# Merging the inverted 32-blocks: four heads in one product of 128 rows instead of two heads in one of 64, for a linear-attention and mixture-of-experts kernel

## The chip, the cores and the metric

The kernel runs on one core of one Trainium2 chip, as a single program. The metric is the device time of an execution in microseconds (us); lower is better. The time of a kernel is the median of its runs.

## The reference

The reference has two parts. The first is a recurrence with a 40x40 state for each of 4 batches and 8 heads over 768 time steps, all in float32:

```python
for t in range(S):                                   # 768 steps
    y[:, :, t] = einsum('bhd,bhde->bhe', rt, state)
    Sa = einsum('bhde,bhe->bhd', state, at)
    state = state * wt[:, :, None, :] - einsum('bhd,bhe->bhde', Sa, bt) \
            + einsum('bhd,bhe->bhde', vt, kt)
```

The second takes its output as a matrix x of 3072 tokens by 320, computes gate logits `x @ w_gate` (320x8), turns their exponentials into a matrix P by eight rounds of row and column normalisation, and adds up, over 8 experts, `P[:, e] * (relu(x @ w1[e]) @ w2[e])` with a hidden width of 1024.

## The kernel before, in words

The kernel has two stages. `attention` computes the recurrence and writes x to device memory; `body` then runs the experts. Only `attention` is changed.

**Chunks.** Time is cut into 12 chunks of 64 steps (`NCH`, `C`). A chunk is handled for the 4 batches one after the other; the 8 heads of a batch are 4 pairs (`NP`), a pair occupying rows 0 to 39 and 64 to 103 of a tile. `prep` (L110) loads a chunk and batch, scales k, b and a by running products of the decay, forms the 64x64 matrices of inner products on TensorE (`ll`, L154) and writes the strictly triangular part that has to be inverted to device memory (`lt` to `ld`, L157 or L173).

**The inverse.** The recurrence inside a chunk needs, for each batch and head, the inverse T of a 64x64 unit triangular matrix. Chunks are taken in six groups of two (`GROUPS`). For a group, `load_lu` (L368) brings the two diagonal 32x32 blocks of all its matrices into VectorE's layout, `inv_diag` to `inv_16` invert them on VectorE, and `finish` (L362) writes the inverted blocks to device memory, straight (`ud`, L365) and transposed (`nd`, L366). The upper right 32x32 block of T is then the product of the first inverted block, the off-diagonal block and the second inverted block. This merge is what is changed.

**The merge.** `tload(c)` (L228) issues ten DMAs on SP's queue for a chunk: two for the off-diagonal blocks (`lb`, L238), two for the transposed first block (`t1`, L241), two for the second block (`t2`, L243), and four that put both inverted blocks on the diagonal of `tt` (L247). A pair of heads is held block-diagonally in 64 rows and 64 columns; 16 pairs (4 batches by 4 pairs) stand beside each other along the free axis. `tmat(c, half)` (L249) runs twice for a chunk, each time for 8 pairs, that is two batches: 8 products of a 64x64 stationary with 32 moving columns into `gp` (L256), two ScalarE copies from `gp` onto the diagonal of `gs` (L257, L258), 8 products of the same shape into `op` (L261), and two ScalarE copies into the upper right blocks of `tt` (L262, L263). `lb` and `gs` are the lower and the upper 64 partitions of one tile, and so are `t1` and `t2`.

**The recurrence.** `recur(c, b)` (L265) is a generator of five steps: products `av` (L283), `xc` (L291), `pu` (L302, whose stationary operand is `tt`), `c2` (L309), and the transpose `zt` (L329) of the new state, with VectorE, ScalarE and GpSimd work between them. `gate` (L336) adds the gate logits of a finished chunk, four products of 64 stationary and 8 moving columns (`lp`, L339), which `gate_step` (L347) puts between the `xc` products.

**The order.** Each piece of work gets a due time in a list `ev` (L378 to L412), and is emitted in the order of these times: step k of chunk c and batch b at 5c + k + 1.1b, `tload(c)` at 5c - 0.5, and `tmat` of the first half at 5c, of the second half at 5c + 2.2. Within the attention stage the framework then orders the instructions of each engine itself, from these priorities and from its own estimate of when each can start; from the ninth block of the experts on the order is the program's. Each engine works through its own queue in order. `gp`, `op` and `lp` share two accumulator banks (tag `pt`). `tt` has two buffers, the tile of `t1` and `t2` and that of `lb` and `gs` one each.

**The experts.** `layer1` (L579, products `p` at L577, hi and lo parts of split operands) and `layer2` (L634, products `op` at L642) run in 128 blocks; the change does not touch them.

Of the kernel before, what the change touches and what calls it, by code (L numbers as in the profile page):

```python
# [11 lines left out]
F32 = mybir.dt.float32  # L12
# [8 lines left out]
NP = 4  # L21
# [7 lines left out]
def attention(ctx, tc, d, xd, ps, pq, pt, gs, lg):  # L29
    nc = tc.nc  # L30
# [3 lines left out]
    const = ctx.enter_context(tc.tile_pool(name="a_const", bufs=1))  # L34
# [15 lines left out]
    for n in range(NCH * NB - NSX, NCH * NB):  # L50
        i, pool = n % NSX, sets[n - NCH * NB + NSX]
# [8 lines left out]
        bb_b[i] = pool.tile([128, NP, 104], F32, name=f"bb{i}")  # L60
        cc_b[i] = pool.tile([R2, NP], F32, name=f"cc{i}")
    tt_b = [const.tile([128, 4 * NP, 128], F32, name=f"tt{i}") for i in range(NTB)]
    td_b = [const.tile([128, 4 * NP, 32], F32, name="td")]
    lg_b = [const.tile([128, 4 * NP, 64], F32, name="lg")]
    ab_b = [pin.tile([R2, NP, 128], F32, name=f"ab{i}") for i in range(2)]
    g1_b = [pin.tile([R2, NP, 65], F32, name=f"g1{i}") for i in range(1)]
    vz_b = [const.tile([R2, NP, 104], F32, name=f"vz{i}") for i in range(5)]
    c1_b = [const.tile([R2, NP, 104], F32, name=f"c1{i}") for i in range(2)]
# [15 lines left out]
    def clear():  # L84
        nc.gpsimd.memset(unf, 0.0)
        nc.gpsimd.memset(unf[:, 0:1024:33], 1.0)
        nc.gpsimd.memset(tnf, 0.0)
        for t in vz_b + c1_b + lg_b:
            nc.vector.memset(t, 0.0)
        for t in tt_b:  # L90
            nc.gpsimd.memset(t, 0.0)
# [11 lines left out]
    def rot(key, lst):  # L103
        i = state[key]
        state[key] = (i + 1) % len(lst)
        return lst[i]
# [121 lines left out]
    def tload(c):  # L228
        tt = rot("tt", tt_b)
        tts[c] = tt  # L230
        ld, ud, nd = invs[GRP[c][0]]
        t1, t2, lb = td_b[0][0:64], td_b[0][64:128], lg_b[0][0:64]
        cc = GRP[c][1]
        q = [slice(h * 32, h * 32 + 32) for h in range(2)]
        u = [[slice(cc * 64 + blk * 32 + h * 16, cc * 64 + blk * 32 + h * 16 + 16) for h in range(2)]
             for blk in range(2)]
        for h in range(2):
            nc.sync.dma_start(out=lb[q[h], :, q[h]],  # L238
                              in_=ld[cc, 0:32].rearrange("j b p h s -> j (b p) h s")[:, :, h, 32:64])
        for h in range(2):  # L240
            nc.sync.dma_start(out=t1[q[h]], in_=nd[u[0][h]].rearrange("g j s -> j g s"))  # L241
        for h in range(2):
            nc.sync.dma_start(out=t2[q[h]], in_=ud[u[1][h]].rearrange("g j s -> j g s"))  # L243
        for h in range(2):
            for blk in range(2):
                r = slice(h * 64 + blk * 32, h * 64 + blk * 32 + 32)
                nc.sync.dma_start(out=tt[r, :, r], in_=ud[u[blk][h]].rearrange("g j s -> j g s"))  # L247

    def tmat(c, half):  # L249
        gl = slice(half * 8, half * 8 + 8)  # L250
        tt = tts[c][:, gl]
        t1, t2 = td_b[0][0:64, gl], td_b[0][64:128, gl]
        lb, gs = lg_b[0][0:64, gl], lg_b[0][64:128, gl]
        gp = pt.tile([64, 2 * NP, 32], F32, name="gp", tag="pt")
        for p in range(2 * NP):
            nc.tensor.matmul(gp[:, p], lhsT=lb[:, p], rhs=t1[:, p], start=True, stop=True)  # L256
        nc.scalar.copy(out=gs[0:32, :, 0:32], in_=gp[0:32])  # L257
        nc.scalar.copy(out=gs[32:64, :, 32:64], in_=gp[32:64])  # L258
        op = pt.tile([64, 2 * NP, 32], F32, name="op", tag="pt")
        for p in range(2 * NP):  # L260
            nc.tensor.matmul(op[:, p], lhsT=gs[:, p], rhs=t2[:, p], start=True, stop=True)  # L261
        nc.scalar.copy(out=tt[0:32, :, 32:64], in_=op[0:32])  # L262
        nc.scalar.copy(out=tt[64:96, :, 96:128], in_=op[32:64])  # L263

    def recur(c, b):  # L265
        pp = preps[c, b]
# [89 lines left out]
    preps, invs, tts = {}, {}, {}  # L356
# [33 lines left out]
    for c in range(NCH):  # L390
        for b in range(NB):
            for k in range(5):
                ev.append((5 * c + k + SKEW * b, step, (c, b)))
        t = 5 * c + 2 - T_LEAD
        ev.append((t - L_LEAD, tload, (c,)))
        for half in range(2):
            ev.append((t + 2 * SKEW * half, tmat, (c, half)))
    for s, cs in enumerate(GROUPS):
        us = slice(0, 64 * len(cs))
        t0 = 5 * cs[0] - 10  # L400
# [24 lines left out]
SKEW = 1.1  # L425
# [35 lines left out]
def body(ctx, tc, d, out):  # L461
# [377 lines left out]
```

## Time and profile before

| | us |
|---|---|
| median of 3 runs | 1874.04 |
| lowest, highest run | 1859.17, 1875.54 |
| the profiled execution | 1873.12 |
| its span, first to last instruction | 1871.3 |
| TensorE matmul busy | 1777.2 |
| VectorE busy | 1373.9 |
| ScalarE busy | 856.0 |
| GpSimd busy | 868.1 |

The span lies 1.8 us below the time of its own execution. PE is TensorE's matmuls, PEld its loads of the stationary operand, DVE VectorE, ACT ScalarE, POOL GpSimd, SP the engine that issues most DMAs. Every float32 product of the attention stage stands in the trace as two matmul instructions with a weight load each. A row of the timeline gives the start, the time from the first start to the last end, the engine, the line, the tiles, the shape (128*104 is 128 rows and 104 columns of the stationary operand; 128x104 after it is the moving operand) and the count of merged instructions. A matmul lasts 0.2 to 0.3 us from its start to its end, but the next can start much sooner, so the distance between starts is what a product costs. PEclk is the share of TensorE's clock that was granted.

### The profile page before, as it was taken

Reading aid. Unit: us, or ns where it says so; the run is one execution under the profiler, and the core shown is the slowest. Engines: PE = TensorE matmul, PEld = TensorE weight load, DVE = VectorE, ACT = ScalarE, POOL = GpSimd, SP = SyncE. Lnnn points to the kernel's source line nnn. Section 1 sums busy time; section 2 is a strip of 40 time slices with the busy share of each in tenths; the row PEclk is TensorE's granted clock in tenths of the full one; section 3 lists DMA queues with packets and bytes.
Section 4 is the critical chain, followed back from the end, with each engine's and each line's share of the span. In section 5 each row is a group of like instructions: output and inputs, shape, how many; then the busy total and the mean of one; then the engine's idle time right before and its main releaser. Section 6 shows DMA issues by size and latency. Waiting matters only on the chain.

```text
span 1871.3 us, 32059 instructions
## 1 busy us (share of the span) xinstructions
PE 1777.2 (95%) x12035; PEld 1735.4 (93%) x12035; DVE 1373.9 (73%) x2378; ACT 856.0 (46%) x1848; POOL 868.1 (46%) x849
## 2 busy tenths in 40 slices
PE   4479999999999999999999999999999999999999
PEld 4468889889988899999999999999999999999999
DVE  6885958756389877676877768886776867767675
ACT  6346767654563434344343434344343434434342
POOL 6544646431265337182643718005371835538170
PEclk8568989977879999999999999999999999999999
DMA  8477877873741111020111102211110201102011
GB/s 190 115 152 156 176 169 183 170 149 80 171 127 45 37 37 55 20 74 19 56 37 37 56 19 74 59 30 37 37 58 17 74 19 56 40 35 67 8 37 43
DMA packets 214048, 141.47 MB, mean 76 GB/s; under 512 B 177157, under 2 KB 191493, under 8 KB 213893
## 3 DMA queue, kind: packets, MB, share of 16 engines
q1 hardware_dynamic: 210693, 134.18, 28.1%
q10 hardware_dynamic: 3200, 5.25, 1.1%
q8 instruction: 95, 1.56, 0.4%
q14 instruction: 60, 0.49, 0.1%
HBM read 113.82 MB, written 25.56 MB: 74 GB/s over the span
## 4 chain that ended last, share of the span: by engine, by line
PE 77%; DVE 5%; DMA 3%; POOL 1%; issue 1%; SPq 1%; ACT 1%; DVEq 0%; POOLq 0%; ACTq 0%
PE op L642 35%; PE p L577 33%; PE xc L291 2%; PE pu L302 1%; PE av L283 1%; PE lp L339 1%; DVE hl L601 1%; PE c L309 1%; PE ll L154 1%; PE op L261 1%; PE gp L256 1%; DMA ld<-lt 1%; DMA inp<-in_inp_dram 1%; DVE sm L595 1%; PE zt L329 1%
## 5 line engine op out<-in xcount | busy, mean ns | idle before, releaser
L577 PE MATMUL p<-xch,wh 128*128 128x384 f32 (+1 forms) x1792 | 605.6, 339 | 6.1 <-DVE u L595 2.2
L598 ACT ACTIVATE hh<-sm 128x384 fp32r<-128x384 f32 x512 | 269.5, 527 | 728.9 <-DVE sm L595 728.9
L642 PE MATMUL op<-wh,hh 128*128 128x320 f32 x1536 | 476.8, 311 | 1.1 <-ACT hh L598 0.9
L642 PE MATMUL op<-wl,hh 128*128 128x320 f32 x1536 | 474.5, 309 | 0.0
L642 PE MATMUL op<-wh,hl 128*128 128x320 f32 x1536 | 467.6, 310 | 1.3 <-DVE hl L601 1.3
L523 POOL TENSOR_TENSOR wl<-ws,wh 128x640 fp32r<-128x640 f32 x60 | 103.1, 1718 | 605.9 <-ACT wh L521 605.7
L601 DVE SCALAR_TENSOR_TENSOR hl<-sm,hh 128x384 fp32r<-128x384 f32 x512 | 375.4, 766 | 2.7 <-ACT hh L598 2.2
L577 PEld LDWEIGHTS p<-xch,wh 128*128 128x128 f32 (+1 forms) x1792 | 337.2, 188 | 9.8 <-DVE u L595 3.8
L577 PE MATMUL p<-xcl,wh 128*128 128x384 f32 x896 | 302.6, 338 | 0.0
L577 PE MATMUL p<-xch,wl 128*128 128x384 f32 x896 | 301.9, 337 | 0.0
L642 PEld LDWEIGHTS op<-wh,hh 128*128 128x128 f32 x1536 | 290.2, 189 | 2.0 <-ACT hh L598 1.9
L642 PEld LDWEIGHTS op<-wl,hh 128*128 128x128 f32 x1536 | 291.0, 189 | 0.0
L642 PEld LDWEIGHTS op<-wh,hl 128*128 128x128 f32 x1536 | 286.9, 188 | 2.1 <-DVE hl L601 2.0
L595 DVE TENSOR_TENSOR sm<-p,u 128x384 f32<-128x384 f32 x384 | 234.5, 621 | 9.2 <-PE p L577 0.5
L577 PEld LDWEIGHTS p<-xcl,wh 128*128 128x128 f32 x896 | 168.7, 188 | 0.0
L577 PEld LDWEIGHTS p<-xch,wl 128*128 128x128 f32 x896 | 168.6, 188 | 0.0
L595 DVE TENSOR_TENSOR sm<-p,p 128x384 f32<-128x384 f32 x128 | 71.2, 557 | 128.6 <-PE p L577 71.9
L595 DVE TENSOR_TENSOR p<-p,p 128x384 f32<-128x384 f32 x128 | 71.1, 555 | 101.6 <-PE p L577 100.2
L313 POOL TENSOR_TENSOR y<-ws,gl 104x256 f32<-104x256 f32 x48 | 42.8, 892 | 153.9 <-DVE ws L311 92.2
L595 DVE TENSOR_TENSOR u<-p,p 128x384 f32<-128x384 f32 x128 | 70.8, 553 | 57.0 <-PE p L577 55.9
L531 POOL TENSOR_TENSOR wl<-ss,wh 128x512 fp32r<-128x512 f32 x60 | 90.4, 1506 | 29.0 <-ACT wh L528 24.8
L154 PE MATMUL ll<-ab,kb 104*128 104x128 f32 x336 | 61.7, 341 | 40.7 <-POOL kb L142 16.2
(161 smaller groups left out, 2823.8 us busy)
## 6 DMA issues: line engine op xcount, KB each, us to landing
ws<-in_wts_dram SPq DMA_DIRECT2D x60, 832.0 KB
inp<-in_inp_dram SPq DMA_DIRECT2D x42, 419.2 KB
rb<-in_r_dram SPq DMA_DIRECT2D x48, 208.0 KB
ld<-lt ACTq DMA_DIRECT2D x40, 128.0 KB
vz<-in_v_dram SPq DMA_DIRECT2D x48, 104.0 KB
gd<-g SPq DMA_DIRECT2D x48, 104.0 KB
gl<-gd SPq DMA_DIRECT2D x48, 104.0 KB
f<-in_vt_dram SPq DMA_DIRECT2D x48, 80.0 KB
```

Source lines behind the costliest of these rows:

```text
L154: nc.tensor.matmul(ll[:, p], lhsT=kb[:, p], rhs=ab[:, p], start=True, stop=True)
L256: nc.tensor.matmul(gp[:, p], lhsT=lb[:, p], rhs=t1[:, p], start=True, stop=True)
L261: nc.tensor.matmul(op[:, p], lhsT=gs[:, p], rhs=t2[:, p], start=True, stop=True)
L291: nc.tensor.matmul(xc[h][:, p], lhsT=pp["sx"][:, p, h], rhs=f[:, p, h], start=True, stop=True)
L313: nc.gpsimd.tensor_tensor(out=y, in0=ws[:, :, 0:64], in1=gl, op=ALU.mult)
L523: g.tensor_tensor(out=wl[:, 0:640], in0=raw[:, 256:896], in1=wh[:, 0:640], op=ALU.subtract)
L531: g.tensor_tensor(out=lv[:, 3:7], in0=so[:, :, 0], in1=hv[:, 3:7, 0], op=ALU.subtract)
L577: nc.tensor.matmul(o, lhsT=w_, rhs=x_, start=(j == 0), stop=(j == 3))
L595: eng.tensor_tensor(out=out, in0=x, in1=y, op=ALU.add)
L598: nc.scalar.activation(out=hh[:, f, h], in_=sm[f][:, h], func=AF.Relu)
L601: v.scalar_tensor_tensor(out=hl[:, f, h], in0=sm[f][:, h], scalar=0.0, in1=hh[:, f, h], op0=ALU.max, op1=ALU.subtract)
L642: nc.tensor.matmul(ops[i], lhsT=a[:, h, cs], rhs=w_[:, cw], start=(f == 0 and h == 0 and j == 0), stop=(last and h == 1 and j == 2))
```

## The change

The merge handles four heads in one product. A product now has a 128x128 block-diagonal stationary operand: four diagonal 32x32 blocks, namely two heads of a pair in batches 0 and 1 (x = 0) and the two heads of the pair with the same place in batches 2 and 3 (x = 1). Eight products instead of sixteen cover a chunk in each of the two steps, and `tmat(c)` runs once, at the due time of the former first half. The tiles `t1`, `t2` have 128 partitions and half as many columns; `lb` and `gs` are now one and the same tile, whose diagonal blocks are overwritten by the copies out of `gp`. Each of the two steps has four copies of the same size as before instead of two in each of two halves. `tload` issues sixteen DMAs instead of ten: twelve that carry half as much each in place of six, and the four of `tt` unchanged.

```diff
-    td_b = [const.tile([128, 4 * NP, 32], F32, name="td")]
-    lg_b = [const.tile([128, 4 * NP, 64], F32, name="lg")]
+    t1_t, t2_t = (const.tile([128, 2 * NP, 32], F32, name=x) for x in ("t1", "t2"))
+    lb_t = gs_t = const.tile([128, 2 * NP, 128], F32, name="lb")
...
     def tload(c):
...
-        for h in range(2):
-            nc.sync.dma_start(out=lb[q[h], :, q[h]],
-                              in_=ld[cc, 0:32].rearrange("j b p h s -> j (b p) h s")[:, :, h, 32:64])
-        for h in range(2):
-            nc.sync.dma_start(out=t1[q[h]], in_=nd[u[0][h]].rearrange("g j s -> j g s"))
-        for h in range(2):
-            nc.sync.dma_start(out=t2[q[h]], in_=ud[u[1][h]].rearrange("g j s -> j g s"))
+        lv = ld[cc, 0:32].rearrange("j b p h s -> j (b p) h s")
+        for x in range(2):
+            for h in range(2):
+                r = q[2 * x + h]
+                nc.sync.dma_start(out=lb_t[r, :, r], in_=lv[:, x * 8:x * 8 + 8, h, 32:64])
+        for t, src, blk in ((t1_t, nd, 0), (t2_t, ud, 1)):
+            for x in range(2):
+                for h in range(2):
+                    o = u[blk][h].start + x * 8
+                    nc.sync.dma_start(out=t[q[2 * x + h]], in_=src[o:o + 8].rearrange("g j s -> j g s"))
         for h in range(2):
             for blk in range(2):
                 r = slice(h * 64 + blk * 32, h * 64 + blk * 32 + 32)
                 nc.sync.dma_start(out=tt[r, :, r], in_=ud[u[blk][h]].rearrange("g j s -> j g s"))
 
-    def tmat(c, half):
-        gl = slice(half * 8, half * 8 + 8)
-        tt = tts[c][:, gl]
-        t1, t2 = td_b[0][0:64, gl], td_b[0][64:128, gl]
-        lb, gs = lg_b[0][0:64, gl], lg_b[0][64:128, gl]
-        gp = pt.tile([64, 2 * NP, 32], F32, name="gp", tag="pt")
+    def tmat(c):
+        tt = tts[c]
+        q = [slice(i * 32, i * 32 + 32) for i in range(4)]
+        gp = pt.tile([128, 2 * NP, 32], F32, name="gp", tag="pt")
         for p in range(2 * NP):
-            nc.tensor.matmul(gp[:, p], lhsT=lb[:, p], rhs=t1[:, p], start=True, stop=True)
-        nc.scalar.copy(out=gs[0:32, :, 0:32], in_=gp[0:32])
-        nc.scalar.copy(out=gs[32:64, :, 32:64], in_=gp[32:64])
-        op = pt.tile([64, 2 * NP, 32], F32, name="op", tag="pt")
+            nc.tensor.matmul(gp[:, p], lhsT=lb_t[:, p], rhs=t1_t[:, p], start=True, stop=True)
+        for r in q:
+            nc.scalar.copy(out=gs_t[r, :, r], in_=gp[r])
+        op = pt.tile([128, 2 * NP, 32], F32, name="op", tag="pt")
         for p in range(2 * NP):
-            nc.tensor.matmul(op[:, p], lhsT=gs[:, p], rhs=t2[:, p], start=True, stop=True)
-        nc.scalar.copy(out=tt[0:32, :, 32:64], in_=op[0:32])
-        nc.scalar.copy(out=tt[64:96, :, 96:128], in_=op[32:64])
+            nc.tensor.matmul(op[:, p], lhsT=gs_t[:, p], rhs=t2_t[:, p], start=True, stop=True)
+        for x in range(2):
+            for h in range(2):
+                nc.scalar.copy(out=tt[h * 64:h * 64 + 32, x * 8:x * 8 + 8, h * 64 + 32:h * 64 + 64], in_=op[q[2 * x + h]])
...
-        for half in range(2):
-            ev.append((t + 2 * SKEW * half, tmat, (c, half)))
+        ev.append((t, tmat, (c,)))
```

More of the change, by code (lines that the diff above doesn't have):

```diff
@@ L87, in clear @@
         nc.gpsimd.memset(tnf, 0.0)
-        for t in vz_b + c1_b + lg_b:
+        for t in vz_b + c1_b + [lb_t]:
             nc.vector.memset(t, 0.0)
@@ L231, in tload @@
         ld, ud, nd = invs[GRP[c][0]]
-        t1, t2, lb = td_b[0][0:64], td_b[0][64:128], lg_b[0][0:64]
         cc = GRP[c][1]
-        q = [slice(h * 32, h * 32 + 32) for h in range(2)]
+        q = [slice(i * 32, i * 32 + 32) for i in range(4)]
         u = [[slice(cc * 64 + blk * 32 + h * 16, cc * 64 + blk * 32 + h * 16 + 16) for h in range(2)]
              for blk in range(2)]
-        for h in range(2):
-            nc.sync.dma_start(out=lb[q[h], :, q[h]],
-                              in_=ld[cc, 0:32].rearrange("j b p h s -> j (b p) h s")[:, :, h, 32:64])
-        for h in range(2):
-            nc.sync.dma_start(out=t1[q[h]], in_=nd[u[0][h]].rearrange("g j s -> j g s"))
-        for h in range(2):
-            nc.sync.dma_start(out=t2[q[h]], in_=ud[u[1][h]].rearrange("g j s -> j g s"))
+        lv = ld[cc, 0:32].rearrange("j b p h s -> j (b p) h s")
[8 more added lines that the diff above has]
+                    nc.sync.dma_start(out=t[q[2 * x + h]], in_=src[o:o + 8].rearrange("g j s -> j g s"))
         for h in range(2):
@@ L247, in tload @@
                 nc.sync.dma_start(out=tt[r, :, r], in_=ud[u[blk][h]].rearrange("g j s -> j g s"))
-    def tmat(c, half):
-        gl = slice(half * 8, half * 8 + 8)
-        tt = tts[c][:, gl]
-        t1, t2 = td_b[0][0:64, gl], td_b[0][64:128, gl]
-        lb, gs = lg_b[0][0:64, gl], lg_b[0][64:128, gl]
-        gp = pt.tile([64, 2 * NP, 32], F32, name="gp", tag="pt")
+    def tmat(c):
+        tt = tts[c]
+        q = [slice(i * 32, i * 32 + 32) for i in range(4)]
+        gp = pt.tile([128, 2 * NP, 32], F32, name="gp", tag="pt")
         for p in range(2 * NP):
-            nc.tensor.matmul(gp[:, p], lhsT=lb[:, p], rhs=t1[:, p], start=True, stop=True)
-        nc.scalar.copy(out=gs[0:32, :, 0:32], in_=gp[0:32])
-        nc.scalar.copy(out=gs[32:64, :, 32:64], in_=gp[32:64])
-        op = pt.tile([64, 2 * NP, 32], F32, name="op", tag="pt")
+            nc.tensor.matmul(gp[:, p], lhsT=lb_t[:, p], rhs=t1_t[:, p], start=True, stop=True)
+        for r in q:
+            nc.scalar.copy(out=gs_t[r, :, r], in_=gp[r])
+        op = pt.tile([128, 2 * NP, 32], F32, name="op", tag="pt")
         for p in range(2 * NP):
-            nc.tensor.matmul(op[:, p], lhsT=gs[:, p], rhs=t2[:, p], start=True, stop=True)
-        nc.scalar.copy(out=tt[0:32, :, 32:64], in_=op[0:32])
-        nc.scalar.copy(out=tt[64:96, :, 96:128], in_=op[32:64])
+            nc.tensor.matmul(op[:, p], lhsT=gs_t[:, p], rhs=t2_t[:, p], start=True, stop=True)
+        for x in range(2):
+            for h in range(2):
+                nc.scalar.copy(out=tt[h * 64:h * 64 + 32, x * 8:x * 8 + 8, h * 64 + 32:h * 64 + 64], in_=op[q[2 * x + h]])
     def recur(c, b):
```

## The prediction

> **What bounds the kernel now.** The page first, then the table by stretches (from and to, length, busy us of PE, PEld, DVE, ACT and POOL, granted clock, share of the DMA engines busy, GB/s): which engine is full where the changed work stands.
>
> ```profile
> PE 1777.2 (95%) x12035; PEld 1735.4 (93%) x12035; DVE 1373.9 (73%) x2378; ACT 856.0 (46%) x1848; POOL 868.1 (46%) x849
> ```
>
> ```profile
> 120.00:300.00 180.00, 169.75 (x1492) 157.22 (x1491) 137.18 (x237) 117.94 (x297) 94.96 (x113) 0.88 0.78 166
> 300.00:400.00 100.00, 92.28 (x909) 85.56 (x908) 77.59 (x136) 73.50 (x186) 54.04 (x68) 0.99 0.83 180
> 400.00:545.00 145.00, 141.78 (x1124) 131.83 (x1124) 81.12 (x143) 72.98 (x173) 43.30 (x49) 0.76 0.52 128
> ```
>
> All merges lie before 545 us; the experts after it stay as they are. From 120 to 545 us PE is busy 404 of 425 us, but often at half clock: a granted share of 0.88 over 180 us, 0.99 over 100 and 0.76 over 145 means, if the clock is either full or half, 43 + 2 + 70 = 115 us at half. The chain through these 425 us says less:
>
> ```profile
> by line: PE xc L291 9.4%; PE pu L302 5.9%; PE av L283 5.7%; issue 4.2%; PE c L309 4.1%; PE lp L339 3.8%; PE ll L154 3.2%; PE op L261 2.9%; PE gp L256 2.9%; DMA ld<-lt 2.9%; DMA inp<-in_inp_dram 2.6%; PE zt L329 2.3%; DMA vz<-in_v_dram 2.3%;
> ```
>
> PE's entries add up to 40%, `gp` and `op` together to 5.8%, 25 us. So a microsecond taken off PE is worth 0.4 (chain) to 0.95 (busy share); I take 0.65.
>
> **Products.** The merge now:
>
> ```profile
> L256 PE MATMUL gp<-td,lg 64*64 64x32 f32 x384 | 34.3, 236 | 5.8 <-DMA td<-ud 3.0 <-DMA td<-nd 2.8
> ...
> L261 PE MATMUL op<-td,lg 64*64 64x32 f32 x384 | 29.2, 229 | 1.1 <-ACT lg L258 1.1
> ```
>
> ```profile
> 290.21 0.61 PE L291 MATMUL xc<-f,sx 104*104 104x104 f32 x4
> 290.75 0.28 PE L339 MATMUL lp<-gs,y 104*64 104x8 f32 x2
> 290.96 1.12 PE L283 MATMUL av<-rb,vz 104*104 104x128 f32 x8
> 292.01 1.11 PE L256 MATMUL gp<-td,lg 64*64 64x32 f32 x16
> 293.06 0.54 PE L329 MATMUL zt<-cst,z 104*40 104x104 f32 x4
> ...
> 295.43 1.06 PE L302 MATMUL pu<-x,tt 128*128 128x104 f32 x8
> ```
>
> A run of 16 `gp` instructions lasts 1.11 us, the last one about 0.23 (mean of the group), so the starts are (1.11 - 0.23) / 15 = 59 ns apart. Both steps of a chunk are 768 / 12 = 64 instructions, 3.75 us. Afterwards there are 32, with 128 stationary and 32 moving columns, a shape that the trace lacks. Its cost lies between 59 ns (if only the moving columns counted) and that of `pu`, with 128 stationary and 104 moving: (1.06 - 0.28) / 7 = 112 ns. The nearest row has 128 stationary and only 8 moving:
>
> ```profile
> 586.09 0.34 PEld L685 LDWEIGHTS cp<-cl,ones 128*128 128x128 f32 x2
> 586.35 0.19 PEld L642 LDWEIGHTS op<-wh,hh 128*128 128x128 f32 x1
> 586.46 0.19 PEld L642 LDWEIGHTS op<-wl,hh 128*128 128x128 f32 x1
> ```
>
> The second `cp` load starts at 586.09 + 0.34 - 0.19 = 586.24, the next at 586.35, then 586.46: 0.11 us per load whatever moves. I take 112 ns: 32 x 0.112 = 3.58 us. Half as many products at twice the price save 0.17 us a chunk, 2 us in 12.
>
> Two rules of the Trainium skill stand against each other here, both on "TensorE: Matmul & The Clock Gate". "LDWEIGHTS (loading the stationary operand)" has the load grow with the stationary columns, columns over 1.2 in ns: estimates of 107 and 53, beside 112 and 59 in the rows. "Back-to-back issue gap" gives one floor for 1 to 64 moving columns; by that alone halving the products would halve the time. The second is a rival below.
>
> **Switches.** `av` to `gp`: the last `av` (some 0.27 us long, as `pu` is) starts about 290.96 + 1.12 - 0.27 = 291.81, the first `gp` 0.20 us later, where `av`'s own distance is (1.12 - 0.27) / 7 = 0.12. Out again: the last `gp` starts at 292.01 + 1.11 - 0.23 = 292.89, `zt` 0.17 later instead of 0.06. So a visit to the 64-row, 64-column shape costs some 0.19 us over the steady rates, and a run as wide as its neighbours should cost none. There are 48 such runs if unsplit, more where they are cut (x8 at 422.11 below); beside `lp`, narrow itself, nothing is saved. Bounds 0 and 72 visits (13.7 us); I take 52: 10 us.
>
> PE sum: -12 us; at 0.4 to 0.95 that is -5 to -11 (with the bounds on the switches -1 to -15). I take **-8**.
>
> **Clock.** One fall of the clock in single 3.4 us stretches, and the products in them:
>
> ```profile
> 422.22:425.64 3.42, 3.42 (x38) 3.28 (x38) 3.39 (x7) 1.29 (x4) 0.84 (x2) 1.00 0.28 44
> 425.64:429.05 3.41, 3.41 (x37) 3.10 (x38) 2.04 (x5) 3.07 (x8) 0.30 (x1) 1.00 0.76 170
> 429.05:432.46 3.41, 3.41 (x22) 3.10 (x21) 2.49 (x5) 0.87 (x3) 0.00 (x0) 0.50 0.52 104
> ```
>
> ```profile
> 422.11 0.69 PE L256 MATMUL gp<-td,lg 64*64 64x32 f32 x8
> 422.73 0.54 PE L329 MATMUL zt<-cst,z 104*40 104x104 f32 x4
> 423.10 0.90 PE L309 MATMUL c<-pm,st 128*104 128x104 f32 x8
> 423.83 1.06 PE L302 MATMUL pu<-x,tt 128*128 128x104 f32 x8
> 424.73 0.90 PE L291 MATMUL xc<-f,st 104*104 104x104 f32 x8
> 425.55 1.11 PE L261 MATMUL op<-td,lg 64*64 64x32 f32 x16
> 426.60 0.40 PE L339 MATMUL lp<-gs,y 104*64 104x8 f32 x4
> 426.93 0.61 PE L291 MATMUL xc<-f,st 104*104 104x104 f32 x4
> 427.47 0.28 PE L339 MATMUL lp<-gs,y 104*64 104x8 f32 x2
> 427.68 0.61 PE L291 MATMUL xc<-f,st 104*104 104x104 f32 x4
> 428.22 0.28 PE L339 MATMUL lp<-gs,y 104*64 104x8 f32 x2
> 428.43 1.05 PE L283 MATMUL av<-rb,vz 104*104 104x128 f32 x6
> ```
>
> PE never paused, yet the clock was halved at 429.05. What differs is the columns streamed: the first stretch has about 6x32 + 28x104 = 3100 moving columns, the second 14x32 + 8x8 + 8x104 + 6x128 = 2110. It seems that some 2100 columns in 3.4 us are too few. The advice of the Trainium skill on the page named above ("Why this matters for your kernels") is that gaps in PE's work of over 3 us halve the clock; the trace differs, with 3.41 of 3.41 us busy. Afterwards a run of 16 takes 16 x 0.112 = 1.79 us for its 512 columns; the other 1.62 us at `xc`'s 104 columns per 0.09 us (its row at 424.73: (0.90 - 0.26) / 7) carry 1870, in all 2380: still above, but four `lp` with their switches (0.4 us for 32 columns) make it about 1950. Before, one run and four `lp` leave 1.9 us, in all about 2720. So each run comes closer to a fall, but there are half as many. Bounds: a third of the 115 us fewer or more, each us at half clock worth half a us: -19 to +19. I take 0.
>
> **DMA issue.** SP's rows (min/median/max in ns):
>
> ```profile
> L238 SPq DMA_DIRECT2D lg<-ld x24: 599/618/2884, 44.4 to 492.5; - x24
> L241 SPq DMA_DIRECT2D td<-nd x24: 313/487/1443, 108.0 to 494.1; - x24
> L243 SPq DMA_DIRECT2D td<-ud x24: 303/482/1381, 109.2 to 497.5; - x24
> ```
>
> Six issues of 0.48 to 0.62 us become twelve with half the content, at 0.30 (the minima) to 0.62: from 0.4 us to 3.2 us more of SP per chunk; at 0.40, near the minima, 12 x 0.40 - 3.17 = +1.6 us. In place it counts where PE waits for these loads:
>
> ```profile
> 393.15 4.25 DMA td<-nd
> ...
> 476.04 3.16 DMA td<-nd
> ```
>
> Two more issues ahead of the last `t1` are 0.8 us, twice on the chain; `vz`, `gl` and `inp` queue behind the rest. I take **+2** (bounds 0 and 10). That `lb` must now wait for `op` instead of `gp` I cost at nothing: a chunk lasts some 36 us ((545 - 118) / 12), a step 7 us, and the only run of `op` is over long before the next load is due, 4.5 steps later. If it were late, SP would stand still there, with `inp`, `vz` and `gl` of the next steps queued behind, and PE would meet a late `td` load as at 393.15, some 4 us a chunk.
>
> **Order and latency.** The second half's runs and copies move 2.2 steps earlier on PE and ScalarE, ahead of the recurrence steps of batches 0 to 2 that were due between; PE does them 15 us sooner, not more often. From the landing of `t1` to the first columns of `tt` there are now two runs longer by 0.85 us each and two more copies of 0.36 us ahead of `op`, 2.4 us in all. I cost this at nothing from the second chunk on: `tmat` is due two steps, 14 us, ahead of its first `pu`, and PE has the recurrence of the chunk before to work on. If that cover were gone it would be 11 x 2.4 = 27 us. The two accumulator banks shared with `lp` are held longer by each `gp` and `op`, but half as often: nothing.
>
> **First chunk.** Here nothing else is ready:
>
> ```profile
> 111.47 1.88 PE L256 MATMUL gp<-td,lg 64*64 64x32 f32 x16 [2.00 <-DMA td<-ud]
> ...
> 114.44 1.59 PE L261 MATMUL op<-td,lg 64*64 64x32 f32 x13 [1.09 <-ACT lg L258]
> ...
> 116.39 0.36 ACT L262 COPY tt<-op 32x256 f32<-32x256 f32 x1 [2.00 <-PE op L261]
> ...
> 117.58 2.03 PE L302 MATMUL pu<-x,tt 128*128 128x104 f32 x8
> ```
>
> Each run of 16 takes 1.7 us more at half clock, the copies to `gs` 2 x 0.36 more: up to 4.1 us, plus 0.8 of issues. The second half's runs are then done already, so 0 to 4.9; I take **+2.5**. ScalarE's copies keep their number and size.
>
> **Sum:** 1873.1 - 8 + 2 + 2.5 + 0 = 1869.6, say 1870 us, 0.2% under the median of 1874.0, which the profiled execution all but equals. Its own range is 1856 to 1890.
>
> **Rivals.** (1) PE is the bound throughout, and falls go with the number of runs: -11 - 19 + 4.5 = 1848 us. For it: PE's 404 of 425 us; against: 40% on the chain. Chance 0.24. (2) The deeper runs win: with a gate step nearby each drops the clock. It becomes slower by 1% once half-clock time grows by (18.7 + 3.5) x 2 = 44 us, to some 160; at 65 us more, +32, the time is 1902. For it: the fall shown, and that a run of 16 at half clock (16 x 0.21 = 3.4 us, 0.21 being twice 0.112) would fill a whole such stretch with 512 columns. Against: half as many runs. Chance 0.23. (3) The edit does what it says, a wide product costing what a narrow one does: 12 x 32 x (0.112 - 0.059) = 20 us less of PE, x 0.65 = 13, so 1857. For it: nothing in the trace; against: the `cp` loads 0.11 apart. It is what the floor of the Trainium skill's "Back-to-back issue gap" would give. Chance 0.05, mostly on the faster side.
>
> **Numbers.** Forecast 0.48. Within 1% is about what a measurement can tell from no change. Faster 0.27 (rival 1 and part of 3), same 0.50, slower 0.23. Range 1845 to 1897.
>
> **What would show it.** Right: `gp` and `op` at 128*128, x192 each, starts 112 ns apart, no pause before or after them; 96 copies as before; the time of the clock at half near 115 us. Wrong: starts near 60 ns; half-clock time under 80 or over 160 us; `td` loads (then `t1`, `t2`) on the chain for more than the two chunks.

## The result, and the profile after

| | before | after |
|---|---|---|
| median of 20 runs each, taken together (us) | 1858.7 | 1880.13 |
| lowest, highest run | 1843.18, 1875.54 | 1870.34, 1892.12 |
| the profiled execution | 1873.12 | 1884.71 |
| its span | 1871.3 | 1882.9 |

The ratio is 1.0132, 95% interval 1.0113 to 1.0152: the change makes the kernel 1.3% slower, some 24.5 us by this ratio (the medians in the table differ by 21.4 us). The forecast of 1870 had the direction wrong: it took 3.5 us off its base, and the change added 21 to 25. Its range held the time. The profiled execution of before, on which the sum stands, lies 14 us above the median of the 20 runs, so the spans of the two traces differ by only 11.6 us.

The page of after, first the busy time of the engines, then the table by stretches (from and to, length, busy us of PE, PEld, DVE, ACT and POOL, granted clock, DMA share, GB/s):

```profile
PE 1755.5 (93%) x11651; PEld 1724.1 (92%) x11651; DVE 1370.4 (73%) x2378; ACT 858.3 (46%) x1848; POOL 874.0 (46%) x849
```

```profile
120.00:300.00 180.00, 157.43 (x1310) 149.92 (x1309) 135.08 (x234) 114.73 (x287) 97.23 (x109) 0.86 0.74 158
300.00:400.00 100.00, 88.96 (x745) 84.70 (x744) 70.67 (x128) 66.94 (x169) 53.70 (x65) 0.86 0.77 175
400.00:545.00 145.00, 132.52 (x1108) 126.25 (x1108) 84.15 (x150) 83.08 (x199) 44.54 (x51) 0.84 0.57 138
```

From 120 to 545 us TensorE is busy 157.4 + 89.0 + 132.5 = 378.9 us, before 403.8, so 24.9 us less. Not all of this is the wide products: the kernel before with only its loads cut in two (below) is busy 390.0 us here, 13.8 less than before, with products unchanged. The stretch has a fixed length, so what busy time loses, idle time gains; whether anything came of it shows in the end of the recurrence. The last `c` products of the recurrence, before:

```profile
543.77 0.98 PE L309 MATMUL c<-pm,bb 128*104 128x104 f32 x8 [2.15 <-DVE pm L304]
```

and after:

```profile
542.98 1.72 PE L310 MATMUL c<-pm,bb 128*104 128x104 f32 x8 [3.20 <-DVE pm L305]
```

They end at 544.8 and 544.7 us: with less work on TensorE the recurrence was through no sooner. The 11.6 us between the two traces appear behind it, where the experts take over (545 to 600 us, before and after):

```profile
545.00:600.00 55.00, 50.44 (x282) 46.47 (x280) 46.62 (x82) 23.96 (x48) 29.89 (x27) 0.91 0.22 62
```

```profile
545.00:600.00 55.00, 43.58 (x233) 39.36 (x232) 43.25 (x71) 21.22 (x39) 33.89 (x34) 0.84 0.23 71
```

The 51st `op` product of the experts starts at 569.5 us before and at 581.1 after, and the lag stays at 11.6 us from there on. Half-clock time from 120 to 545 us is 50 + 28 + 46 = 125 us, before 115.

What the recurrence waited for, in spite of the cheaper products, stands in the chain through its stretch. The first fence is the chain of after by line (the view cuts the row at its length), the second its longest pieces on the load of a chunk's inputs (start, us):

```profile
by line: PE xc L292 10.3%; DMA inp<-in_inp_dram 8.0%; PE pu L303 7.0%; PE av L284 6.5%; issue 5.6%; PE c L310 5.2%; DMA ld<-lt 4.9%; PE ll L154 4.5%; PE lp L340 3.3%; PE op L261 2.8%; ACT x L298 2.5%; ACT c L299 2.5%; PE zt L330 2.3%; ACT l
```

```profile
263.41 5.41 DMA inp<-in_inp_dram
299.28 4.88 DMA inp<-in_inp_dram
340.48 5.89 DMA inp<-in_inp_dram
383.14 6.38 DMA inp<-in_inp_dram
392.25 6.74 DMA inp<-in_inp_dram
```

`inp` had 2.6% of the 425 us before (11 us) and has 8.0% now (34 us). It is not a load that the change touches. It stands behind the touched ones in SP's queue. SP's rows of after from one `inp` to the next (start, us from the first start to the last end, line, transfer, count):

```profile
232.10 0.99 SPq L113 DMA_DIRECT2D inp<-in_inp_dram  x2
...
243.67 2.40 SPq L240 DMA_DIRECT2D lb<-ld  x3
246.12 0.44 SPq L245 DMA_DIRECT2D t<-nd  x1
...
247.85 1.50 SPq L245 DMA_DIRECT2D t<-nd  x3
249.39 2.16 SPq L245 DMA_DIRECT2D t<-ud  x4
251.60 0.98 SPq L249 DMA_DIRECT2D tt<-ud  x2
...
263.41 0.58 SPq L113 DMA_DIRECT2D inp<-in_inp_dram  x1
```

and at the same chunk before:

```profile
231.57 0.55 SPq L113 DMA_DIRECT2D inp<-in_inp_dram  x1
...
250.52 0.59 SPq L113 DMA_DIRECT2D inp<-in_inp_dram  x1
```

31 us pass between these two `inp` issues instead of 19. The lag doesn't stay that large: the `inp` issue behind them comes at 265.70 us instead of 261.88, and the last of all at 392.25 instead of 381.10. Who waits for `inp` is in the waits from 120 to 545 us (engine, what and line, for what; us in all, times, longest), first after, then before:

```profile
POOL kb L142 <- DVE q L119: 73.7, 6, 17.3
...
DVE q L119 <- DMA inp<-in_inp_dram: 25.9, 13, 5.4
```

```profile
POOL kb L142 <- DVE q L119: 24.8, 4, 13.0
...
DVE q L119 <- DMA inp<-in_inp_dram: 15.7, 12, 3.4
```

`prep` of the next group starts with the scan `q` on VectorE, GpSimd scales `kb` with it, and a late `inp` stops both. What it does to the recurrence shows in the rows of GpSimd, VectorE and PE of after:

```profile
190.10 1.48 POOL L142 TENSOR_TENSOR kb<-inp,q 104x512 f32<-104x512 f32 x1 [14.81 <-DVE q L119]
...
194.87 0.73 POOL L314 TENSOR_TENSOR y<-ws,gl 104x256 f32<-104x256 f32 x1
195.56 0.90 POOL L325 TENSOR_TENSOR z<-ws,st 104x160 f32<-104x160 f32 x1
```

```profile
189.27 0.70 DVE L119 TENSOR_TENSOR_SCAN q<-inp,cst 104x260 f32<-104x260 f32 x1 [1.45 <-DMA inp<-in_inp_dram]
...
192.06 0.56 DVE L312 TENSOR_TENSOR ws<-c,c 104x416 f32<-104x416 f32 x1
```

```profile
192.68 1.12 PE L284 MATMUL av<-rb,vz 104*104 104x128 f32 x8 [2.04 <-DVE ws L312]
...
196.51 0.88 PE L330 MATMUL zt<-cst,z 104*40 104x104 f32 x4 [0.87 <-POOL z L325]
```

Most of GpSimd's 14.8 us seems to cost nothing by itself. But when `inp` is there at last, the work of `prep` falls into the middle of a running step: `ws` stands behind `q` and the scan after it on VectorE, `y`, which needs the `ws` that ends at 192.62, starts 2.2 us later behind `ab`, `z` after it, and PE waits twice. In the middle the recurrence runs late: the first `pu` of the fifth chunk starts at 277.64 us instead of 258.87, that of the ninth at 431.64 instead of 414.42. But it makes this good, for that of the twelfth starts at 512.83 instead of 517.20. Nor are the later inverses held up: `finish` begins to write `ud` of the third group at 224.94 us instead of 235.17, of the last at 451.50 instead of 469.79.

### The profile page after: what moved, and what is told of

Same layout as the page of the kernel before. It is cut to its first block, busy times and chain, and to the rows that moved or that the text cites. A ratio compares the mean times of both kernels' runs of the same rounds, so it can differ in the third digit from the quotient of the medians.

```text
span 1882.9 us, 31391 instructions
## 1 busy us (share of the span) xinstructions
PE 1755.5 (93%) x11651; PEld 1724.1 (92%) x11651; DVE 1370.4 (73%) x2378; ACT 858.3 (46%) x1848; POOL 874.0 (46%) x849
## 4 chain that ended last, share of the span: by engine, by line
PE 78%; DVE 5%; DMA 5%; ACT 3%; SPq 2%; issue 1%; POOL 0%; ACTq 0%; DVEq 0%; POOLq 0%
PE op L642 35%; PE p L577 32%; PE xc L292 2%; DMA inp<-in_inp_dram 2%; PE pu L303 2%; PE av L284 1%; DMA ld<-lt 1%; PE c L310 1%; PE ll L154 1%; PE lp L340 1%; PE op L261 1%; DVE sm L595 1%; ACT x L298 1%; ACT c L299 1%; DVE hl L601 1%
## 5 line engine op out<-in xcount | busy, mean ns | idle before, releaser
L601 DVE SCALAR_TENSOR_TENSOR hl<-sm,hh 128x384 fp32r<-128x384 f32 x512 | 369.8, 756 | 2.8 <-ACT hh L598 2.4
```

What stands on the lines that cost most here:

```text
L601: v.scalar_tensor_tensor(out=hl[:, f, h], in0=sm[f][:, h], scalar=0.0, in1=hh[:, f, h], op0=ALU.max, op1=ALU.subtract)
```

## The experiments

Two theories stood against each other at first. Theory "loads": the six further DMA issues a chunk are the price. Theory "merge": the wide products, or the merge at one point instead of two, are. Each ratio below is to the kernel before, run on the same chip, with its 95% interval.

**The loads alone.** The kernel before, its six loads cut into twelve; products and due times untouched:

```diff
-        for h in range(2):
-            nc.sync.dma_start(out=t1[q[h]], in_=nd[u[0][h]].rearrange("g j s -> j g s"))
+        for x in range(2):
+            for h in range(2):
+                o = u[0][h].start + x * 8
+                nc.sync.dma_start(out=t1[q[h], x * 8:x * 8 + 8], in_=nd[o:o + 8].rearrange("g j s -> j g s"))
...
```

> The kernel before with one part of the change: the six loads of lb, t1 and t2 cut into twelve of half the size; products, copies and due times as before. If the six further issues per chunk make the change slow (they cost SP some 2 us per chunk in the trace of after: 4 x 0.396 + 8 x 0.448 us instead of 3.2), this shows most of the 1.3%: 1.008 to 1.015 of before. If the merge of all batches at one point or the wide products make it slow, 0.997 to 1.003. If it is only that any edit shuffles the order that the framework finds, anything from 0.99 to 1.01.

Measured: 1878.32 us, 1.0146 (1.0099 to 1.0193). That is the whole loss of the change, without any of its products.

**The merge at one point alone.** The kernel before with both halves of `tmat` due at once:

```diff
-            ev.append((t + 2 * SKEW * half, tmat, (c, half)))
+            ev.append((t, tmat, (c, half)))
```

> The kernel before with another part alone: both halves of the merge get the due time of the first, so all batches of a chunk are merged together, still with 64-row products and ten loads. If merging all batches at one point (PE and ScalarE work moved ahead of the steps of batches 0 and 1) makes the change slow, 1.008 to 1.015 of before. If the loads or the wide products do, 0.997 to 1.003. If only the order is shuffled, anything from 0.99 to 1.01.

Measured: 1849.24 us, 0.9976 (0.9948 to 1.0004). Moving the second half earlier costs nothing.

**Wide products in two halves**, four products of 128 rows at each of the old due times, with the sixteen loads:

```diff
-        ev.append((t, tmat, (c,)))
+        for half in range(2):
+            ev.append((t + 2 * SKEW * half, tmat, (c, half)))
```

> The wide products alone in time as before: four heads in 128 rows, but two halves of four products each at the two old due times (the four heads are two neighbouring pairs of one batch), with sixteen loads and sixteen copies of half the size. If the loads make the change slow, as slow as after: 1.010 to 1.016 of before. If merging all batches at one point does, it is faster than before by the 30 us of PE work that the change takes off, weighted: 0.990 to 0.998. Only the order: 0.99 to 1.01.

Measured: 1882.78 us, 1.0145 (1.0109 to 1.0181). The point of the merge is not the price.

**Wide products with half the loads.** After, with the loads for x = 0 only: it leaves out the blocks of batches 2 and 3 in the merge, and issues ten DMAs a chunk.

```diff
-        for x in range(2):
+        for x in range(1):
```

> The changed kernel with only the loads for x = 0: ten DMAs a chunk as before, in place of sixteen, with half the bytes of lb, t1 and t2; the blocks of two batches are left out of the merge (zeros stand in their place), products and copies run as in the change. If the further loads make the change slow, it comes back to before or below: 0.99 to 1.00. If it is the merge at one point or the wide products, it stays at 1.010 to 1.015. Only the order: anything from 0.99 to 1.015.

Measured: 1851.17 us, 0.997 (0.9942 to 0.9997). "Merge" falls, "loads" holds. But the bytes were halved too; three more kernels parted number from size.

**Wide products, ten loads, all bytes.** The matrices of a chunk are put in the order batch, pair, head in device memory, so that `t1` and `t2` come in one DMA each; the reads of the diagonal blocks become four a group instead of eight.

```diff
+        nc.sync.dma_start(out=t1_t, in_=nd[u[0]].rearrange("(g x) j s -> (x j) g s", x=4))
+        nc.sync.dma_start(out=t2_t, in_=ud[u[1]].rearrange("(g x) j s -> (x j) g s", x=4))
```

> The changed kernel with its wide products, but ten loads a chunk: the 64 systems of a chunk and block stand in the order (batch, pair, head), and the four heads of a product are two neighbouring pairs of a batch, so that one load brings all 128 rows of t1 and one those of t2; load_lu needs four transfers a group instead of eight. Same result, same bytes. If the number of loads is what the change pays for and the wide products are even, it is at or under before: 0.985 to 1.000. If the wide products or the merge at one point cost something after all, 1.003 to 1.013.

Measured: 1859.85 us, 1.0003 (0.9973 to 1.0033).

**The same order with narrow products**, eight loads a chunk:

> The kernel before with 64-row products and its two due times, with the same order of systems: eight loads a chunk instead of ten, and four transfers instead of eight for load_lu. If the time goes with the number of loads (six more a chunk cost 1.4 to 1.7%, here it is four fewer), 0.985 to 0.995. If before had room on its queues and only a burst above some limit costs, 0.996 to 1.003.

Measured: 1853.49 us, 0.9976 (0.9945 to 1.0007). With the number of loads brought down, the wide products gain nothing over the narrow ones.

**Six tiny loads.** The kernel before with six loads of 4 KB a chunk on SP's queue, between those of `t2` and of `tt`, into a tile that nothing reads:

```diff
+        for i in range(6):
+            nc.sync.dma_start(out=dm[i], in_=ud[u[i // 3][0].start + i])
```

> The kernel before with six further loads a chunk on SP, each 32x32 of the inverted blocks (4 KB) into a tile that nobody reads, right behind those of t2. Everything else as before. If the count of issues on SP is the cost, as slow as with the loads cut in two: 1.008 to 1.016. If it is the smaller pieces in which the merge's own operands arrive, 0.997 to 1.003.

Measured: 1888.69 us, 1.0169 (1.0124 to 1.0214). The number counts, not what is carried.

**Where they are issued.** The same six tiny loads on ScalarE's queue, then on GpSimd's:

> The kernel before with the six tiny loads a chunk on ScalarE's queue instead of SP's (on SP they cost 1.7%). If SP's time at the issue is the price, it mostly goes: 1.000 to 1.005, for ScalarE's own 2 us a chunk. If it is the number of transfers in flight, whoever issues them (the program lets every transfer of SP and ScalarE wait for the one eight before it), it stays: 1.010 to 1.017.

Measured: 1876.27 us, 1.0097 (1.0064 to 1.013).

> The same six tiny loads on GpSimd's queue, which issues transfers by a path of its own. If SP's time or the eight transfers in flight of SP and ScalarE are the price, 0.998 to 1.005 plus what GpSimd's issues cost its own work (6 x about 1 us of an engine that is half idle). If the DMA engines or the framework's order are the price, 1.010 to 1.017 here too.

Measured: 1867.83 us, 1.0053 (1.0018 to 1.0088). The rows of these issues (min/median/max in ns), on ScalarE, on GpSimd and, in the kernel of the six tiny loads, on SP:

```profile
L246 ACTq DMA_DIRECT2D dm<-ud x72: 308/324/1141, 103.9 to 474.6; - x72
```

```profile
L246 POOL DMA_DIRECT2D dm<-ud x72: 496/496/685, 104.1 to 467.9; - x72
```

```profile
L246 SPq DMA_DIRECT2D dm<-ud x72: 302/419/2378, 110.3 to 495.0; - x72
```

An issue takes longest on GpSimd, 0.50 us, and costs the end least: 0.0053 x 1860 / 72 = 0.14 us; on ScalarE 0.32 us and 0.25; on SP 0.42 us and 0.0169 x 1859 / 72 = 0.44. On SP alone the whole issue time comes out at the end. But the first of the two forecasts failed for the theory of SP's time: on ScalarE at most 1.005 was to be left, and 1.0097 was. SP's time at the issue is thus not the whole price; it mostly goes on GpSimd only.

**Burst or number.** The tiny loads on SP's queue again, but due one at a time, 0.8 of a due step apart:

```diff
+        for i in range(6):
+            ev.append((t - L_LEAD + 0.8 * (i + 1), tiny, (c, i)))
```

> The kernel before with six loads of 4 KB a chunk on SP's queue, as in the run of the six tiny loads (1.0169), but due one at a time, 0.8 of a due step apart through the chunk, instead of in the burst of the merge's loads. Theory A (each issue costs SP's time wherever it stands, because SP's queue is the bound of the group's chain): 1.013 to 1.020. Theory B (the price is the burst: the loads behind it in the queue, inp above all, come late): 1.000 to 1.006.

Measured: 1895.87 us, 1.0224 (1.017 to 1.0279). The burst isn't the price: spread out they cost no less. The ratio lies above theory A's range, but the intervals of the two forms overlap.

**Three and twelve.**

> The kernel before with three tiny loads a chunk in the burst instead of six. If the price goes by the number of issues from the first one on: half of 1.0169, 1.008. If there is room for some issues and the price begins above it (eight loads were worth no more than ten): under 1.004. If it is any disturbance of the order: as six, 1.014 or more.

Measured: 1868.03 us, 1.0051 (1.0021 to 1.0082).

> The kernel before with twelve tiny loads a chunk in the burst. Price by the number: twice 1.0169, 1.030 to 1.036. Price by the order that the framework finds: anything, most likely 1.015 to 1.025.

Measured: 1917.64 us, 1.0328 (1.0285 to 1.037). In us for each issue: 0.0051 x 1860 / 36 = 0.26, then 0.44 for six, 0.0328 x 1860 / 144 = 0.42 for twelve. From six on the price goes by the number, at the row's 0.42; whether the first three have some room isn't clear, since the interval holds both. In these kernels GpSimd's wait from above grows with it: 24.8 us before, 32.3 with three, 48.7 with six, and with twelve (120 to 545 us; its lines are one further down):

```profile
POOL kb L143 <- DVE q L120: 85.5, 6, 19.1
```

**Loads of the changed kernel on other queues.** First `lb` and `t2` (eight loads) on ScalarE's queue, then `inp` from the ninth on, then the four of `tt`:

> The changed kernel with its eight loads of lb and t2 issued from ScalarE's queue instead of SP's; number, size and content of the sixteen loads stay. If SP's queue is what the further loads cost (SP then issues eight a chunk, fewer than before's ten), the loss is gone: 0.990 to 1.000 of before. If it is the number of transfers or their small pieces in the DMA engines, it stays at 1.010 to 1.016. The ScalarE queue, 46% busy, gets 8 x 0.4 us a chunk more.

Measured: 1871.61 us, 1.0084 (1.0052 to 1.0116).

> The changed kernel with sixteen loads on SP, but the load inp of each chunk and batch from the ninth on is issued from ScalarE's queue. If what is late next is inp, queued behind the sixteen loads on SP (in the trace of after one is issued at 232.1 and the next at 263.4 us, with the loads between), the loss is gone: 0.990 to 1.002. If SP is late for everything (gl, vz, lu) and inp has no special part, 1.005 to 1.012. If SP has no part, 1.010 to 1.016.

Measured: 1872.41 us, 1.0085 (1.0057 to 1.0114).

> A smaller dose: the changed kernel with only the four loads of tt on ScalarE's queue, so that SP issues twelve a chunk, two more than before. If the loss goes with the issues on SP (six more cost 1.3 to 1.5%), about a third of it stays: 1.000 to 1.006. If transfers in the DMA engines cost it, 1.010 to 1.016. If the loads that PE waits for first (lb, t1, t2) matter and not the queue's length, 1.008 to 1.015.

Measured: 1880.14 us, 1.013 (1.009 to 1.0171). ScalarE's queue gives back a third at best, less than the prices of the tiny loads would give (8 x 12 x (0.44 - 0.25) = 18 us for the first). The second forecast came out as it would if `inp` had no special part (1.005 to 1.012). The last is a miss for the theory of SP's time: with twelve issues a chunk on SP, 1.000 to 1.006 was expected, and the whole loss stayed.

**Six of the sixteen on GpSimd's queue**: the four of `t2` and two of `t1`, so that SP issues ten a chunk:

```diff
+                    eng = nc.gpsimd if blk or x else nc.sync
+                    eng.dma_start(out=t[q[2 * x + h]], in_=src[o:o + 8].rearrange("g j s -> j g s"))
```

> The changed kernel with six of its sixteen loads (the four of t2 and the two of t1 for batches 2 and 3) on GpSimd's queue, so that SP issues ten a chunk as before. If the change costs its six issues and nothing else, this is what six tiny loads on GpSimd's queue cost the kernel before: 1.005, within 1.002 to 1.009. If SP's issues were not the price: 1.013 as the changed kernel.

Measured: 1865.49 us, 1.0045 (1.0021 to 1.0068), as forecast from the tiny loads. In time, the change is its six issues; the products, the copies and the merge at one point add nothing to it that can be measured. `kb` hardly waits for `q` any more (120 to 545 us; 73.7 in after):

```profile
POOL kb L142 <- DVE q L119: 3.1, 1, 3.1
```

**A version that beats both?** Eight loads, narrow products, both halves at once:

> Narrow products with eight loads a chunk (t1 and t2 in one each, the reads of the two diagonal blocks in four a group), and both halves of the merge due at once: the two edits that each measured 0.9976. If both are small gains of their own: 0.995. If both are nothing: 0.998 to 1.002.

Measured: 1854.98 us, 0.9985 (0.996 to 1.001): not told from before.

The durations of all of SP's issues before 560 us, added up, the time that SP waited for transfers from 118 to 500 us, and the ratio:

| kernel | issues on SP | their us | waits, us | ratio |
|---|---|---|---|---|
| narrow, eight loads | 575 | 346 | 14 | 0.9976 |
| wide, ten loads | 598 | 353 | 16 | 1.0003 |
| before | 622 | 361 | 19 | 1 |
| three tiny | 658 | 378 | 22 | 1.0051 |
| after | 694 | 380 | 27 | 1.0132 |
| loads split | 688 | 381 | 23 | 1.0146 |
| six tiny | 686 | 399 | 15 | 1.0169 |
| tiny, spread | 688 | 397 | 14 | 1.0224 |
| twelve tiny | 737 | 424 | 16 | 1.0328 |
| after, six loads on GpSimd | 628 | 348 | 16 | 1.0045 |
| after, eight loads on ScalarE | 598 | 326 | 59 | 1.0084 |
| six tiny on ScalarE | 620 | 356 | 34 | 1.0097 |
| after, `tt` on ScalarE | 646 | 352 | 49 | 1.013 |

With all loads on SP, 64 us of issue from before upwards (76 over the whole execution, for some of the twelve's lie behind 560 us) become 61 us of time. Below before nothing is won: there the loads are no longer the bound. The last three rows say why SP's issue time alone isn't the price: SP issues for less time than before, and the kernels are slower by 0.8 to 1.3%. There SP waits 34 to 59 us for transfers under way, before 19, so that much of what a load on ScalarE's queue saves at SP's issue comes back as a wait of SP. (Part of these waits is of `lu` for its own data: 8 us of before's 19, 16 of the 49 with `tt` on ScalarE.) With loads on GpSimd the wait doesn't grow. This fits a limit that SP's and ScalarE's transfers share; no run varied such a limit.

## Why the prediction was wrong, step by step

**The failed step** is "DMA issue: I take +2 (bounds 0 and 10)". Count and length of the issues were right. The rows of after:

```profile
L240 SPq DMA_DIRECT2D lb<-ld x48: 302/396/1412, 34.6 to 480.3; - x48
L245 SPq DMA_DIRECT2D t<-nd x48: 303/446/1564, 108.1 to 483.2; - x48
L245 SPq DMA_DIRECT2D t<-ud x48: 312/449/1816, 110.2 to 488.4; - x48
```

4 x 0.396 + 8 x 0.448 = 5.2 us a chunk instead of 3.2: 2.0 more, forecast 1.6, in 12 chunks 24 us. The step counted this time only "in place", where PE waits for the merge's own loads, twice, and put no price on the rest, that `vz`, `gl` and `inp` queue behind. What the runs show in its place: the six further issues alone, with the products untouched, cost 1.0146, 21 to 27 us, the whole loss, against 10 as upper bound. It is as much as the 24 us of issue by these rows (19 by the sum over all of SP's issues, 361 to 380), but that it arrives by `inp` isn't shown. No rival had the issues as its price; the rival of slower, a lower clock, has a part in the result (see the clock).

**The value of PE's time** failed beside it. The sum gave a microsecond off PE 0.65 us. Against the split loads, with as many issues and the old products, PE is busy 390.0 - 378.9 = 11.1 us less from 120 to 545 us, near the 12 forecast. At equal issues that should have shown as -8 us, 0.4%. It is 1.0003 (0.9973 to 1.0033) with ten loads, which excludes this, though SP has two issues a chunk fewer there than before; the other two pairs, 1.0132 against 1.0146 and 1.0045 against 1.0053 on GpSimd, are level too, but their intervals would hold it. What became of the saving shows in the kernel with ten loads. From 120 to 545 us, before and there:

```profile
120.00:545.00 425.00, 403.81 (x3521) 374.61 (x3521) 295.89 (x516) 264.42 (x654) 192.30 (x229) 0.87 0.70 156
```

```profile
120.00:545.00 425.00, 402.16 (x3219) 383.24 (x3220) 297.00 (x528) 270.04 (x665) 194.19 (x231) 0.83 0.69 156
```

302 matmul instructions fewer, and PE as busy as before, at a lower granted clock.

**Products: right.** Both steps have the shape forecast (min/median/max ns; first and last start):

```profile
L256 PE MATMUL gp<-t,lb x192: 195/276/403, 111.9 to 503.2; 128*128 128x32 f32 x192
L261 PE MATMUL op<-t,lb x192: 195/276/423, 117.1 to 507.6; 128*128 128x32 f32 x192
```

and two runs of 16 with their neighbours on PE:

```profile
376.39 1.04 PE L284 MATMUL av<-rb,vz 104*104 104x128 f32 x8
377.26 1.87 PE L261 MATMUL op<-t,lb 128*128 128x32 f32 x16
378.97 0.52 PE L330 MATMUL zt<-cst,z 104*40 104x104 f32 x4
...
410.86 1.63 PE L292 MATMUL xc<-f,st 104*104 104x104 f32 x16
412.32 1.89 PE L256 MATMUL gp<-t,lb 128*128 128x32 f32 x16
```

The starts of `gp` are (1.89 - 0.23) / 15 = 0.11 us apart, as priced, and rival 3, which had the wide product at 0.059, is out. (The 0.23 is the mean duration of the old products.)

**Switches: right.** The last `xc` starts about 410.86 + 1.63 - 0.26 = 412.23, `gp` 0.09 later, `xc`'s own distance: no pause going in. Before, `gp` came 0.20 after an `av` with a distance of 0.12. Here the last `av` starts at 376.39 + 1.04 - 0.27 = 377.16, `op` 0.10 later. The same holds over all visits at full clock in the two traces, by medians: before, going in takes 0.18 to 0.20 us behind `xc`, `av` and `pu`, whose own distances are 0.09 to 0.11, and going out 0.15 instead of 0.06; after, 0.09 to 0.11 going in and 0.11 going out, the products' own distances. Only going out to `lp`, narrow itself, takes 0.21.

**Clock: taken at nothing, and it was not.** From 120 to 545 us the two traces have 125 us at half against 115, inside the step's bounds and far from rival 2's 160. But the traced execution of before had a low granted clock for its kernel, 0.942, where some 110 executions of before on record have a median of 0.950. Over a whole execution, time at half is 2 x (1 - granted clock) x time. Its medians, with as many loads and narrow or wide products:

| loads a chunk | narrow: clock, us at half | wide: clock, us at half |
|---|---|---|
| ten on SP (before on that chip; wide, ten loads) | 0.949, 190 | 0.9405, 221 |
| sixteen on SP (loads split; after) | 0.9455, 205 | 0.941, 222 |
| ten on SP, six on GpSimd (tiny loads; after's) | 0.9505, 185 | 0.945, 205 |

The wide products bring 17 to 31 us more at half clock. At the prediction's half a us for each these are 9 to 15 us, an estimate, about what they were to save on PE. So rival 2's mechanism was there, at less than its size, and is a likely reason why the cheaper products gained nothing. The further loads bring half-clock time too: 227 us with six tiny ones on SP and 249 with twelve. In all, after has 222 us and before 186 (median of all its executions): 36 us, or 18 us of time by the same price, near the step's upper bound of 19. These bounds did not enter the sum's own range of 1856 to 1890. Rival 1 is out: it needed fewer falls of the clock.

The prediction's reading of the fall, that too few moving columns streamed, holds beyond its one case. In all 19 traces the clock is either full or half, and changes in steps of 3.41 us. From 118 to 545 us they have 1733 such steps at full clock, 223 of them followed by half clock. Counting the moving columns of the products started in each step, a line at 1890 columns puts 44 on the wrong side; the best line through PE's busy share (0.66) puts 98 there. 32 falls came after steps in which PE was busy over 95% of the time, with 1392 to 2112 columns, and 101 steps under 80% busy, with 1520 columns or more, kept the full clock. So it is some 1900 columns rather than 2100, and a merge that streams 384 x 32 columns instead of 768 x 32 in nearly the same PE time (57 us busy instead of 63) comes closer to it.

**The wait of `lb` for `op`: right at nothing.** The longest wait of an `lb` issue on SP is 1.8 us, and it is for another transfer:

```profile
SPq L240 <- DMA inp<-in_inp_dram: 3.4, 4, 1.8
```

**Order and latency: right at nothing.** Both halves at once measured 0.9976 with narrow products, and wide products in two halves 1.0145 against 1.0132 at once.

**First chunk: right, size in its bounds.** After's rows on PE:

```profile
111.93 3.60 PE L256 MATMUL gp<-t,lb 128*128 128x32 f32 x16 [2.37 <-DMA t<-nd]
117.14 3.62 PE L261 MATMUL op<-t,lb 128*128 128x32 f32 x16 [1.62 <-ACT lb L258]
121.59 2.04 PE L303 MATMUL pu<-x,tt 128*128 128x104 f32 x8 [0.82 <-ACT tt L264]
```

The first `pu` starts at 121.59 instead of 117.58: 4.0 us later, forecast 2.5 between 0 and 4.9. By the last chunk the recurrence has made it good (above), and the kernels with these products and fewer issues lose nothing by it that can be measured.

**What stays open.** That the number of issues is the price is shown, by dose and by the layout with fewer loads; how it reaches the end is not. After and the twelve tiny loads show the late `inp` and the waiting `kb`, but neither follows the price. `inp` has 4.5% of the chain with the tiny loads spread, the dearer form, and 13.0% with them in a burst; `kb` waits 13.6 us for `q` in the spread form, but 35.1 us with both halves at once, which costs nothing. In the two traces of before and after the recurrence even ends at the same time, and the loss appears in the first blocks of the experts; with the loads split, six tiny and twelve tiny the last `c` ends later, at 551.7, 563.8 and 575.2 us instead of 544.8. Much of the price comes as half-clock time, but whether waits of PE cause it was not parted from the rest. With `inp` on ScalarE's queue 1.0085 of the 1.0132 stays. The framework orders the instructions anew for each kernel, and that order may carry a part. Nor is it settled why SP, which issues 71% of the time from 118 to 500 us before and 81% with twelve tiny loads, counts in full before it is full.

## What to carry to other kernels

Count the issues of a change on each DMA queue and price them in full, by the rows of that queue, when the queue also carries the loads with which the next stage of work begins; here spreading them out didn't help, ScalarE's queue gave back a third at best and GpSimd's two thirds. Of time saved on a full TensorE ask where it will go: here it seems to have come back as half-clock time, so count the moving columns beside the busy time. A wider product that needs more pieces to be put together should get its data laid out so that it needs no more transfers than the narrow one.

## What the runs showed of the hardware

Cutting a load in two shortens its issue on SP by less than half: `lb` went from a median of 0.618 us to 0.396, `t` from 0.487 to 0.446, so two halves cost more than the whole. The same 4 KB load took 0.42 us to issue on SP, 0.32 on ScalarE and 0.50 on GpSimd, and the end paid 0.44, 0.25 and 0.14 us for it. A product with a 128-row, 128-column stationary and 32 moving columns costs 0.11 us, as much as `pu` with 104 moving columns, and nothing for a switch beside products of 104 rows and columns, where a visit to 64 rows and columns costs 0.09 us going in and 0.09 coming out. TensorE's clock was halved after steps of 3.41 us with fewer than some 1900 moving columns (1689 of 1733 steps on the right side of 1890), even where PE was busy throughout.
